# Second inputs of VectorE's selection steps in free PSUM columns, two key copies on ScalarE, zero rows written on chip, x loaded ahead by four columns

## The chip, the cores and the metric

The kernel runs on one core of one Trainium2 chip. The metric is the device time of one execution in microseconds (us), as the median of three runs. The core has TensorE (PE, matrix products, which write only to PSUM), VectorE (DVE), ScalarE (ACT) and GpSimd (POOL), and a queue of DMAs that SyncE (SP) issues in order.

## What is computed

For four sequences of 12,608 positions and 128 channels, a long convolution with a filter that a small network makes, gated by x; then, in each sequence, the 128 positions with the highest gate score pass through one expert and are written back.

```python
h = np.maximum(pos_emb @ w1, 0.0) @ w2 * np.exp(-0.01 * pos)[:, None]
u = x * v
y = irfft(rfft(u, n=2*S, axis=1) * rfft(h, n=2*S, axis=0)[None], n=2*S, axis=1)[:, :S]
a = x * y                                     # B, S, D = 4, 12608, 128
scores = a @ w_gate
for b in range(B):
    top = np.argpartition(-scores[b], 128)[:128]
    e = a[b, top]
    a[b, top] = e + sigmoid(scores[b, top])[:, None] * (np.maximum(e @ moe_w1, 0.0) @ moe_w2)
```

## The kernel before, in words

The Fourier transforms are matrix products of lengths 101 and 250. After a setup that makes the filter's spectrum (h_hid, h_spec; up to about 114 us), a loop takes one step t for four channels of one sequence: 32 steps a sequence (NG = 32), 128 in all. The order of all instructions is written out by hand; each engine works through its own queue in that order, and a framework adds the waits between engines.

In step t, in the order of the code (L1011 ff.): TensorE makes the inverse product of step t−3 (f_i, L254), then the second forward product of step t (dft, L259) into a PSUM tile of two banks, c0 for odd t and c1 for even t (404 of the 512 columns of each bank are used); ScalarE copies one half of it out (L262). TensorE then makes the first forward product of step t+1 (f_s1, L417), which ScalarE copies (L419). VectorE multiplies with the spectrum for step t−1, which still lies in the other PSUM tile (f_m, L431 and L432; f_y, L437 and L438), then combines step t (f_v, L426; f_u, L423). POOL makes sums and differences for f_i (f_sd, L444 and L445), the product x·v of a step ahead (L240) and a combination of results (f_c, L486 and L487). SP loads x and v of step t+4 (L234) and the spectrum (L244). The dft of step t+1 overwrites the PSUM tile from which L437 and L438 of step t−1 read.

After the 32 steps of a sequence comes its x-stage (P1): the last inverse product (L532, L536), the product with x (L547), the gate's weights (L581), and the row sums on ScalarE (L591). The first five blocks of x, eight columns each (420 KB), are loaded ahead into the buffers xa by load_a, one every second step at i%32 = 20, 22, ..., 28, where i = t−3 (LA, L44). 23 of the 128 rows of the xa buffers hold no data; at t=8 two DMAs write zeros from memory into them (460 KB, L1031).

The selection of the 128 rows of a sequence runs behind the steps of the next sequence, as a generator (topk_one, L973) that stands still at each `yield` until a step reaches a hook of that kind: "p" right after the dft, "n" behind it (no operation of its own: it only says that the next operation waits for a later step), "d" four times between L426 and L423, "e" three times at the step's end, after L423. With s = t mod 32 the background of a sequence starts at s=3: late row sums at s=3 and 4; at s=5 the mask (L594, a minimum of scores and table) and the sign step of the keys (L662); at s=6 the xor (L664), the copy of the keys' upper half (L665) and that of the lower half (L743). Then sixteen rounds of counting, one a step: ScalarE counts (L755), TensorE sums over the partitions (L250), VectorE compares (L761). After the eighth, at s=15, low() makes the second key on ScalarE (L746) and VectorE adds the lower half (L748). select (L780) follows: is_gt and is_equal at s=25 (L790, L793), TensorE's count and, at s=26, a copy (L806), a running sum (L808) and a comparison (L811), at s=27 an add (L814), at s=28 a second running sum (L817) and a product (L820), at s=29 two one-column operations in "d" hooks (L835, L837) and two comparisons (L839, L842), at s=30 the matmul of rows that reads L842's result (place, L250). The gather of the rows on POOL's DMA queue stands at a last hook. A running sum is one scan over 126 columns. All inputs of these steps, but sums straight from TensorE, lie in SBUF. For the last sequence (b = 3) the selection runs at the end, with nothing beside it.

f_last (L448) is the last step's spectrum product in two halves, the second of which has its sums on VectorE (L458, L459).

## Time and profile before

| | us |
|---|---|
| median of three runs | 921.66 (918.89 to 922.53) |
| the profiled execution | 915.3 |
| its span, first to last instruction | 913.4 |

| engine | busy, us | share of the span |
|---|---|---|
| TensorE (PE) | 870.1 | 95% |
| VectorE (DVE) | 825.0 | 90% |
| GpSimd (POOL) | 765.2 | 84% |
| ScalarE (ACT) | 620.7 | 68% |

The profile is of one execution. A share is a mean over the setup, the 128 steps, the four x-stages between them and the tail, which have different limits; a view by stretch gives the busy time of each engine in a part of the span. "Idle before" is the time in which an engine stood still ahead of an instruction, and the name behind the arrow is what ended it; "issue" stands for a wait that the profile does not explain. In the names of tiles the numbers are left out: "c" is a PSUM tile of two banks, "a" one of one bank, "arena" the large SBUF tile that holds most buffers.

### The profile page before, as it was taken

What the parts mean: (1) busy time and instruction counts of PE and PEld (TensorE: products, weight loads), DVE (VectorE), ACT (ScalarE), POOL (GpSimd) and SP (SyncE); (2) the same over time, 40 slices, a digit from 0 to 9 for tenths busy, and PEclk for the clock granted to TensorE, in tenths of its full rate; (3) what the DMA queues carried; (4) which work ended last, traced back from release to release, by engine and by line L of the source; (5) the groups of instructions that cost most, each with busy time, mean ns of one, the idle gap of its engine ahead of it and who ended that gap; (6) DMA issues with size and microseconds to landing.
All of it is one profiled execution on the core that took longest, in us unless ns stands there. A gap on an engine that the chain in (4) does not pass through costs nothing.

```text
span 913.4 us, 46302 instructions
## 1 busy us (share of the span) xinstructions
PE 870.1 (95%) x19606; PEld 748.2 (82%) x19606; DVE 825.0 (90%) x1543; ACT 620.7 (68%) x2226; POOL 765.2 (84%) x834
## 2 busy tenths in 40 slices
PE   8999899999999999999999999999999999989965
PEld 6878669899979878889798788887997788968954
DVE  8999799899999899999997999999998989997883
ACT  6665545555549969885579688955697888746920
POOL 5898569999999879898998798988997989979810
PEclk9999999999999999999999999999999999999997
DMA  7144587767879967677789676787797666855910
GB/s 246 39 184 170 193 296 192 248 208 225 256 220 285 306 179 229 194 237 230 234 244 300 208 222 196 229 234 240 231 295 236 203 207 207 249 167 168 296 55 7
DMA packets 80677, 195.52 MB, mean 214 GB/s; under 512 B 9302, under 2 KB 46271, under 8 KB 80447
## 3 DMA queue, kind: packets, MB, share of 16 engines
q1 hardware_dynamic: 80214, 192.04, 66.8%
q8 instruction: 154, 2.52, 1.1%
q0 software_dynamic: 256, 0.52, 0.2%
q14 instruction: 53, 0.43, 0.2%
HBM read 151.93 MB, written 40.60 MB: 211 GB/s over the span
## 4 chain that ended last, share of the span: by engine, by line
PE 53%; DVE 27%; ACT 11%; DMA 4%; issue 3%; POOL 3%; POOLq 0%; DVEq 0%; SPq 0%; ACTq 0%
PE c L254 15%; PE a L417 13%; PE c L259 12%; ACT arena L591 9%; DVE c L432 4%; DVE arena L431 4%; DVE arena L437 3%; DVE c L426 2%; DVE arena L438 2%; DVE c L423 2%; PE c L393 2%; PE a L373 2%; PE c L373 2%; DMA out_dram<-arena 1%; DMA hd<-arena 1%
## 5 line engine op out<-in xcount | busy, mean ns | idle before, releaser
L254 PE MATMUL c<-ci_sb,arena 128*26 128x126 f32 x8128 | 259.4, 270 | 5.3 <-issue 3.8
L254 PEld LDWEIGHTS c<-ci_sb,arena 128*26 128x26 f32 x8128 | 241.7, 104 | 10.1 <-issue 5.9
L259 PE MATMUL c<-arena,cf_sb 128*32 128x404 f32 x2048 | 211.9, 503 | 7.6 <-DVE arena L438 4.2
L417 PE MATMUL a<-c_sb,arena 128*32 128x202 f32 (+1 forms) x4096 | 214.3, 334 | 0.3 <-issue 0.3
L417 PEld LDWEIGHTS a<-c_sb,arena 128*32 128x32 f32 (+1 forms) x4096 | 167.4, 109 | 34.9 <-issue 15.2
L240 POOL TENSOR_TENSOR arena<-arena 128x500 f32<-128x500 f32 x128 | 162.5, 1270 | 12.4 <-DMA arena<-in_xg_dram 12.4
L444 POOL TENSOR_TENSOR arena<-arena 128x404 f32<-128x404 f32 x127 | 123.8, 974 | 54.0 <-DVE arena L438 39.6
L419 ACT COPY arena<-a 128x404 f32<-128x404 f32 x256 | 128.0, 500 | 52.8 <-PE a L417 50.9
L467 ACT COPY big<-c 128x824 f32<-128x824 f32 x127 | 106.3, 837 | 84.3 <-PE c L254 84.0
L591 ACT ACTIVATE arena<-arena 128x128 f32<-128x128 f32 x502 | 147.4, 297 | 11.4 <-DVE arena L581 9.5
L259 PEld LDWEIGHTS c<-arena,cf_sb 128*32 128x32 f32 x2048 | 93.0, 109 | 45.7 <-issue 24.4
L431 DVE TENSOR_TENSOR arena<-c,arena 128x808 f32<-128x808 f32 x127 | 126.6, 997 | 3.6
L432 DVE TENSOR_TENSOR c<-c,arena 128x808 f32<-128x808 f32 x127 | 126.6, 997 | 0.0
L445 POOL TENSOR_TENSOR arena<-arena 128x404 f32<-128x404 f32 x127 | 124.2, 978 | 0.0
L591 ACT ACTIVATION_READ_ACCUMULATOR arena<-arena 128x1 f32 x502 | 94.9, 189 | 0.0
L519 POOL TENSOR_TENSOR arena<-big 128x512 f32<-128x512 f32 x72 | 89.7, 1282 | 0.7 <-PE c L532 0.4
L262 ACT COPY arena<-c 128x404 f32<-128x404 f32 x128 | 63.5, 496 | 39.4 <-PE c L259 35.5
L426 DVE TENSOR_TENSOR c<-c,arena 128x404 f32<-128x404 f32 x128 | 74.6, 583 | 14.4 <-ACT arena L262 11.5
L437 DVE TENSOR_TENSOR arena<-c,arena 128x404 f32<-128x404 f32 x127 | 73.5, 579 | 12.9
L487 POOL TENSOR_TENSOR big<-big,arena 128x184 f32<-128x184 f32 x128 | 74.5, 582 | 10.0
L423 DVE TENSOR_TENSOR c<-c,arena 128x404 f32<-128x404 f32 x128 | 75.0, 586 | 2.7
L486 POOL TENSOR_TENSOR big<-big,arena 128x184 f32<-128x184 f32 x128 | 75.2, 587 | 0.0
(183 smaller groups left out, 1441.4 us busy)
## 6 DMA issues: line engine op xcount, KB each, us to landing
arena<-in_xg_dram SPq DMA_DIRECT2D x256, 250.0 KB, 3.7
arena<-hd SPq DMA_DIRECT2D x128, 404.0 KB, 4.4
arena<-in_x_dram SPq DMA_DIRECT2D x60, 420.0 KB, 4.8
out_dram<-arena SPq DMA_DIRECT2D x60, 420.0 KB, 5.5
hd<-arena SPq DMA_DIRECT2D x32, 404.0 KB, 3.0
arena<-in_pos_dram SPq DMA_DIRECT2D x15, 202.0 KB, 4.3
arena<-in_x_dram SPq DMA_DIRECT2D x4, 315.0 KB, 4.0
out_dram<-arena SPq DMA_DIRECT2D x4, 315.0 KB, 5.2
```

The lines of the kernel that those rows point to most:

```text
L240: nc.gpsimd.tensor_tensor(out=x, in0=x, in1=v, op=ALU.mult)
L254: nc.tensor.matmul(o[32 * k:32 * k + c.stop - c.start], lhsT=lhsT[:, c], rhs=rhs, start=True, stop=True)
L259: nc.tensor.matmul(pq[w][a:a + 32], lhsT=cf_sb[:, 2 * w + a // NQ, a % NQ:a % NQ + 32], rhs=te[:, a // NQ], start=True, stop=True)
L417: nc.tensor.matmul(tps[s // 2][c, s % 2], lhsT=u[:, s, c], rhs=c1_sb[:, 0:k + 2:k + 1], start=True, stop=True)
L419: nc.scalar.copy(out=te[:, :, 2 * h:2 * h + 2].rearrange("p e s i -> p s e i"), in_=tps[h])
L431: nc.vector.tensor_tensor(out=mt, in0=uv, in1=ht[:, 0].unsqueeze(1).to_broadcast([128, 2, HC]), op=ALU.mult)
L432: nc.vector.tensor_tensor(out=uv, in0=uv, in1=ht[:, 1].unsqueeze(1).to_broadcast([128, 2, HC]), op=ALU.mult)
L437: nc.vector.tensor_tensor(out=yz[:, 0], in0=uv[:, 1], in1=mt[:, 0], op=ALU.add)
L444: eng.tensor_tensor(out=nat(sd[:, 0]), in0=nat(yz[:, 0]), in1=rev(yz[:, 1]), op=ALU.add)
L445: eng.tensor_tensor(out=nat(sd[:, 1]), in0=rev(yz[:, 0]), in1=nat(yz[:, 1]), op=ALU.subtract)
L467: nc.scalar.copy(out=ay[:, t % NG, :NJ + JM, ss], in_=o3[:, :, :NJ + JM].rearrange("p s x -> p x s"))
L591: nc.scalar.activation(out=x, in_=x, func=AF.Copy, accum_out=self.sc[:, j:j + 1])
```

## The change

Four things are changed.

First, operands of the selection for the first three sequences are moved from SBUF into PSUM columns that no product uses: `gap(k, n)` is a view of columns 404 to 404+n of both banks of tile c0 or c1, with the 126 columns laid out as two halves. The mask's table is copied there once, at t=2, by ScalarE (c1); the sign step's result, the keys' lower half, the marks of select and one comparison lie in c0. VectorE's operations there then have one input in SBUF and one in PSUM (the sign step: its output in PSUM). A running sum becomes two scans of 63 columns, the second starting from the first's last value.

Second, the copies of the keys' upper and lower halves go from VectorE to ScalarE, in one step with the xor, and a "n" between the sign step and the xor goes away.

Third, the zero rows are no longer loaded: at t=0, 1 and 2 ScalarE writes zeros over the five xa buffers, all 128 rows of 1024 columns. The table `zr` and its argument are gone.

Fourth, the five blocks of x are loaded ahead in ten pieces of four columns, one in each step at i%32 = 20 to 29.

Besides, f_last keeps the second half's difference in PSUM.

```diff
@@ -41,7 +41,7 @@
 NE = 3
-LA = range(32 - 12, 32 - 2, 2)
+LA = range(32 - 12, 32 - 2)
 NS, ND = 64, 4
@@ -139,7 +139,7 @@
-    return (fold.astype(f), c1.astype(f), gx.astype(f), cf.astype(f), ci.astype(f), wm, tk, np.zeros((128 - P0 - PR, NX * 8 * D), f))
+    return (fold.astype(f), c1.astype(f), gx.astype(f), cf.astype(f), ci.astype(f), wm, tk)
@@ -192,6 +192,12 @@
         return view(bank2[k], 0, shape)
...
+    def gap(k, n):
+        return bank2[k].rearrange("p (c x) -> p c x", c=2)[:, :, HC:HC + n]
...
+    def c3(a):
+        return a.rearrange("p (c x) -> p c x", c=2)
@@ -206,6 +212,7 @@
     negm = tk_sb[:, 294:294 + NJ]
+    negp, tmp = gap(1, NJ // 2), gap(0, NQ)
     nst = tk_sb[:, 294 + NJ:].rearrange("p (r c) -> p r c", c=4)
@@ -454,9 +461,10 @@
             nc.vector.tensor_tensor(out=y[:, 0], in0=u[:, 1], in1=m[:, 0], op=ALU.add)
-            nc.vector.tensor_tensor(out=y[:, 1], in0=m[:, 1], in1=u[:, 0], op=ALU.subtract)
-            eng.tensor_tensor(out=d[:, 0], in0=y[:, 0], in1=y[:, 1, :, ::-1], op=ALU.add)
-            eng.tensor_tensor(out=d[:, 1], in0=y[:, 0, :, ::-1], in1=y[:, 1], op=ALU.subtract)
+            z = u[:, 0] if a else y[:, 1]
+            nc.vector.tensor_tensor(out=z, in0=m[:, 1], in1=u[:, 0], op=ALU.subtract)
+            eng.tensor_tensor(out=d[:, 0], in0=y[:, 0], in1=z[:, :, ::-1], op=ALU.add)
+            eng.tensor_tensor(out=d[:, 1], in0=y[:, 0, :, ::-1], in1=z, op=ALU.subtract)
         return sd
@@ -500,13 +508,14 @@
-        def load_a(self, i):
+        def load_a(self, i, a=0, z=8):
             if i < len(ORD):
...
                 j0, j1 = blocks[k]
+                z = min(z, j1 - j0)
                 o = i % (NX + len(XE))
                 self.xa[k] = buf("xa", o, [128, 8, D]) if o < NX else view(arena, XE[o - NX], [128, 8, D])
-                nc.sync.dma_start(self.xa[k][P0:P0 + PR, :j1 - j0], x2[self.b, :, j0:j1])
+                nc.sync.dma_start(self.xa[k][P0:P0 + PR, a:z], x2[self.b, :, j0 + a:j0 + z])
@@ -591,7 +600,8 @@
         def mask(self):
-            nc.vector.tensor_tensor(out=self.sc, in0=self.sc, in1=negm, op=ALU.min)
+            sc, m = (self.sc, negm) if self.last else (c3(self.sc), negp)
+            nc.vector.tensor_tensor(out=sc, in0=sc, in1=m, op=ALU.min)
@@ -714,8 +724,6 @@
                         if not self.ex:
-                            if k == 1:
-                                yield "n"
                             yield "e"
@@ -737,15 +745,23 @@
             self.cand = nst[:, 8]
-            self.lo = buf("ws", 0, [128, self.n])
+            self.lo = gap(0, self.n // 2)
         def split(self):
-            return super().split() + [lambda: nc.vector.tensor_copy(self.lo, self.half(U16, 0))]
+            V, sc, m = nc.vector, c3(self.sc.bitcast(I32)), self.lo.bitcast(I32)
...
+            def keys():
+                V.tensor_tensor(out=sc, in0=sc, in1=m, op=ALU.bitwise_xor)
+                nc.scalar.copy(out=self.key, in_=self.half(I16, 1))
+                nc.scalar.copy(out=self.lo, in_=c3(self.half(U16, 0)))
...
+            return [lambda: V.tensor_scalar(out=m, in0=sc, scalar1=31, scalar2=0x7FFFFFFF, op0=ALU.arith_shift_right,
+                                            op1=ALU.bitwise_and), keys]
...
             yield "e"
-            nc.vector.tensor_tensor(out=self.f, in0=self.f, in1=self.lo, op=ALU.add)
+            nc.vector.tensor_tensor(out=c3(self.f), in0=c3(self.f), in1=self.lo, op=ALU.add)
             self.key, self.cand = self.f, nst[:, 9]
@@ -784,40 +800,46 @@
         sn, rk = ws[:, o:o + n], ws[:, o + 2 * n:o + 3 * n + 2]
-        ev, oh = ws[:, o + n:o + 2 * n], ws[:, 128:256]
+        last = b + 1 == B
+        ev, oh = ws[:, o + n:o + 2 * n] if last else gap(0, n // 2), ws[:, 128:256]
+        w3 = (lambda a: a) if last else c3
         nc.scalar.activation(out=rk[:, n + 1:n + 2], in_=rs, func=AF.Copy, bias=float(b * PR * NJ))
...
+        def scan(initial):
+            for x, y in ((sn, ev),) if last else ((sn[:, h * n // 2:(h + 1) * n // 2], ev[:, h]) for h in range(2)):
+                nc.vector.tensor_tensor_scan(out=x, data0=one.to_broadcast([128, x.shape[1]]), data1=y, initial=initial,
+                                             op0=ALU.mult, op1=ALU.add)
+                initial = x[:, x.shape[1] - 1:]
...
         yield "e"
...
         yield "e"
-        nc.vector.tensor_scalar(out=ev, in0=k.f, scalar1=th, scalar2=0.0, op0=ALU.is_equal, op1=ALU.add,
+        nc.vector.tensor_scalar(out=ev, in0=w3(k.f), scalar1=th, scalar2=0.0, op0=ALU.is_equal, op1=ALU.add,
                                 accum_out=cnt[:, 1:2])
-        if b + 1 == B:
-            nc.vector.tensor_tensor_scan(out=sn, data0=one.to_broadcast([128, n]), data1=ev, initial=0.0, op0=ALU.mult,
-                                         op1=ALU.add)
+        if last:
+            scan(0.0)
         yield "p"
...
         mm2(ps[:, 0:1], tr, cnt[:, 1:2], start=False, stop=True)
-        if b + 1 == B:
+        if last:
             warm(3)
         yield "e"
-        if b + 1 < B:
+        if not last:
             nc.vector.tensor_copy(lim, ps[:, 0:1])
             yield "e"
-            nc.vector.tensor_tensor_scan(out=sn, data0=one.to_broadcast([128, n]), data1=ev, initial=lim,
-                                         op0=ALU.mult, op1=ALU.add)
+            scan(lim)
             yield "e"
-            nc.vector.scalar_tensor_tensor(out=ev, in0=sn, scalar=CAP + 0.5, in1=ev, op0=ALU.is_lt, op1=ALU.mult)
+            nc.vector.scalar_tensor_tensor(out=ev, in0=c3(sn), scalar=CAP + 0.5, in1=ev, op0=ALU.is_lt, op1=ALU.mult)
             yield "n"
             yield "e"
-            nc.vector.tensor_tensor(out=ev, in0=gt, in1=ev, op=ALU.add)
+            nc.vector.tensor_tensor(out=ev, in0=c3(gt), in1=ev, op=ALU.add)
             yield "n"
             yield "e"
-            nc.vector.tensor_tensor_scan(out=sn, data0=one.to_broadcast([128, n]), data1=ev, initial=0.0, op0=ALU.mult,
-                                         op1=ALU.add)
+            scan(0.0)
             yield "e"
-            nc.vector.tensor_tensor(out=rk[:, :n], in0=sn, in1=ev, op=ALU.mult)
+            nc.vector.tensor_tensor(out=c3(rk[:, :n]), in0=c3(sn), in1=ev, op=ALU.mult)
             tot = sn[:, n - 1:n]
@@ -828,18 +850,18 @@
             warm(2)
-            nc.vector.tensor_tensor_scan(out=sn, data0=one.to_broadcast([128, n]), data1=ev, initial=0.0, op0=ALU.mult,
-                                         op1=ALU.add)
+            scan(0.0)
             nc.vector.tensor_tensor(out=rk[:, :n], in0=sn, in1=ev, op=ALU.mult)
...
         yield "e"
-        nc.vector.tensor_scalar(out=ws[:, :128], in0=iot, scalar1=rk[:, n:n + 1], scalar2=0.0, op0=ALU.is_ge,
+        ge, i3 = (ws[:, :128], iot) if last else (tmp, c3(iot))
+        nc.vector.tensor_scalar(out=ge, in0=i3, scalar1=rk[:, n:n + 1], scalar2=0.0, op0=ALU.is_ge,
                                 op1=ALU.add, accum_out=cnt[:, 1:2])
         yield "e"
-        nc.vector.scalar_tensor_tensor(out=oh, in0=iot, scalar=en, in1=ws[:, :128], op0=ALU.is_lt, op1=ALU.mult)
+        nc.vector.scalar_tensor_tensor(out=w3(oh), in0=i3, scalar=en, in1=ge, op0=ALU.is_lt, op1=ALU.mult)
         return rk, oh
@@ -1026,9 +1048,11 @@
             load_u(t + NU)
-            if t == 8:
-                for r, z in ((0, P0), (P0 + PR, 128)):
-                    nc.sync.dma_start(arena[r:z, OFF["xa"][0]:OFF["xa"][0] + NX * 8 * D], zr[:z - r])
+            for k in range(2 * t, min(2 * t + 2, NX)):
+                nc.scalar.activation(out=buf("xa", k, [128, 8 * D]), in_=one.to_broadcast([128, 8 * D]), func=AF.Copy,
+                                     scale=0.0)
+            if t == 2:
+                nc.scalar.copy(out=negp, in_=c3(negm))
             o = t - 1 in uv
@@ -1070,7 +1094,8 @@
                 ph[b] = P1(b)
-            ph[b].load_a(LA.index(i % NG))
+            k, e = divmod(LA.index(i % NG), 2)
+            ph[b].load_a(k, e * HB, (e + 1) * HB)
         if i % NG == NG - 1 and i >= 0:
```

## Rows read from the trace of the kernel before

**Rows 1.** The page's first part: engine, busy us, share of span, instructions.
```profile
...
PE 870.1 (95%) x19606; PEld 748.2 (82%) x19606; DVE 825.0 (90%) x1543; ACT 620.7 (68%) x2226; POOL 765.2 (84%) x834
...
```

**Rows 2.** By stretch, t=12-27: us, PE, PEld, DVE, ACT, POOL busy, clock, DMA, GB/s.
```profile
...
168.25:239.46 71.21, 71.21 (x1797) 66.50 (x1791) 66.16 (x96) 40.87 (x80) 66.28 (x79) 1.00 0.75 224
...
```

**Rows 3.** Busy time by stretch: selection steps, first batch, and sum over three batches.
```profile
...
322.53:342.85 20.32, 18.35 (x465) 14.68 (x460) 19.67 (x33) 13.37 (x37) 15.97 (x19) 1.00 0.57 167
...
374.21:383.49 9.28, 9.28 (x242) 7.79 (x237) 8.95 (x18) 7.42 (x23) 9.12 (x11) 1.00 0.60 194
...
414.87:439.11 24.24, 23.42 (x608) 20.63 (x603) 23.48 (x40) 12.77 (x25) 19.80 (x24) 1.00 0.79 229
...
sum 167.18, PE 157.96 PEld 130.89 DVE 161.79 ACT 104.50 POOL 137.87; mean PE 17.55 PEld 14.54 DVE 17.98 ACT 11.61 POOL 15.32
```

**Rows 4.** Timeline of a plain step: start us, us, engine, line, [idle before <-releaser].
```profile
...
218.81 0.56 DVE L438 TENSOR_TENSOR arena<-arena,c 128x404 f32<-128x404 f32 x1
219.00 0.49 ACT L262 COPY arena<-c 128x404 f32<-128x404 f32 x1 [0.30 <-PE c L259]
...
220.77 1.00 DVE L431 TENSOR_TENSOR arena<-c,arena 128x808 f32<-128x808 f32 x1
...
221.66 0.50 PE L259 MATMUL c<-arena,cf_sb 128*32 128x404 f32 x1
...
```

**Rows 5.** Timeline, TensorE at t=40.
```profile
...
333.39 0.55 PE L259 MATMUL c<-arena,cf_sb 128*32 128x404 f32 x4 [1.70 <-DVE arena L438]
```

**Rows 6.** Timeline around t=62: slots of the selection, and who waits.
```profile
...
433.92 0.15 DVE L835 COPY arena<-a 128x1 f32<-128x1 f32 x1
...
434.05 0.58 DVE L423 TENSOR_TENSOR c<-c,arena 128x404 f32<-128x404 f32 x1
...
434.54 0.34 DVE L839 TENSOR_SCALAR_CACHE_REDUCE arena<-tk_sb,arena 128x128 f32<-128x128 f32 x1
434.60 0.96 POOL L445 TENSOR_TENSOR arena<-arena 128x404 f32<-128x404 f32 x1
...
434.93 0.78 DVE L842 SCALAR_TENSOR_TENSOR arena<-tk_sb,sel,arena 128x128 f32<-128x128 f32 x1
...
435.76 0.43 PE L250 MATMUL a<-arena 128*32 128x64 f32 x16 [0.53 <-DVE arena L842]
...
```

**Rows 7.** VectorE's groups by line and shape | busy us, mean ns | idle before.
```profile
...
L743 DVE CAST arena<-sc 128x126 f32<-128x126 uint16 x3 | 3.9, 1308 | 0.0
...
L811 DVE SCALAR_TENSOR_TENSOR arena<-arena 128x126 f32<-128x126 f32 x3 | 3.5, 1173 | 0.1
...
L808 DVE TENSOR_TENSOR_SCAN arena<-one,sel,arena 128x126 f32<-128x126 f32 x3 | 3.3, 1104 | 0.1
...
L817 DVE TENSOR_TENSOR_SCAN arena<-one,arena 128x126 f32<-128x126 f32 x3 | 1.3, 442 | 0.0
...
```

**Rows 8.** Line L581: duration ns min/median/max, first and last start us, shapes.
```profile
...
L581 DVE TENSOR_TENSOR arena<-arena,c x91: 421/677/680, 274.9 to 866.5; 128x512 f32<-128x512 f32 x88, 128x256 f32<-128x256 f32 x3
...
```

**Rows 9.** Timeline around t=48: low() on ScalarE and VectorE.
```profile
...
369.61 0.40 ACT L746 ACTIVATE f<-hi,st 128x126 f32<-128x126 int16 x1
...
369.75 0.51 PE L259 MATMUL c<-arena,cf_sb 128*32 128x404 f32 x2
...
370.04 0.85 DVE L748 TENSOR_TENSOR f<-f,arena 128x126 f32<-128x126 f32 x1 [1.17 <-ACT f L746]
...
```

**Rows 10.** Busy time by stretch: t=10, and t=88.
```profile
...
157.51:163.79 6.28, 4.90 (x125) 4.45 (x120) 5.87 (x10) 2.56 (x5) 6.20 (x8) 1.00 1.00 323
593.57:599.25 5.68, 4.77 (x126) 4.08 (x117) 5.29 (x11) 3.46 (x11) 5.60 (x7) 1.00 0.95 284
...
```

**Rows 11.** Timeline of TensorE within t=10.
```profile
...
162.91 0.31 PE L254 MATMUL c<-ci_sb,arena 128*25 128x126 f32 x4 [1.38 <-issue]
```

**Rows 12.** Timeline of ScalarE at t=1.
```profile
...
119.90 0.50 ACT L262 COPY arena<-c 128x404 f32<-128x404 f32 x1 [1.68 <-PE c L259]
```

**Rows 13.** VectorE's groups by line and shape, as rows 7: the last step.
```profile
...
L459 DVE TENSOR_TENSOR arena<-arena 128x202 f32<-128x202 f32 x1 | 0.7, 748 | 0.0
...
```

4 lines of the change are left out of this document (2 added, 2 removed).

## The prediction

> **What bounds the kernel now.** I read the page first. TensorE is busy 95% of the span [rows 1], VectorE 90%, GpSimd 84%; so I asked for stages, not shares. A stretch of sixteen steps without background work takes 71.21 us, all of it PE [rows 2]: 4.45 us a step, set by TensorE. VectorE is busy 66.16 us there, 4.13 a step: it runs in time but has only 0.32 us a step to spare, so whatever the selection adds to VectorE is not free, it is a debt paid back at 0.32 us a step.
>
> Then I priced the steps in which the selection runs against 4.45 (s is t mod 32; the background starts at s=3). Nine stretches, 34 steps, take 167.18 us [rows 3]; 34 × 4.45 is 151.3, so 15.9 us is lost there, in the same three places for each of three batches; the first batch's stretches stand as examples: making the keys and the first round (s=6 to 9) 20.32 − 17.80 = 2.5 us, low() with its aftermath (s=17, 18) 9.28 − 8.90 = 0.4, select (s=26 to 30) 24.24 − 22.25 = 2.0. The other two batches lose about 3.0, 0.4 and 2.0.
>
> How a debt becomes lost time: in a plain step [rows 4] L438 ends at 219.37, and the dft that overwrites the same PSUM tile starts two dfts on, 221.66: VectorE may be 2.3 us late before PE waits. After the keys it is later: PE stands 1.70 us for L438 [rows 5]. After the slots it is L842 that PE's row matmul waits for, 0.53 us [rows 6].
>
> Why VectorE is late: the operations are short but stretched. The scan L808 takes 1104 ns, the like scan L817 takes 442; L811 1173, L743 1308 on 126 columns [rows 7]. L842 shows what stretches them: it starts at 434.93 while POOL's L445 runs from 434.60 for 0.96, and ends 0.15 us after that ends [rows 6]. An operation with one PSUM input isn't stretched: 91 of L581 have median 677 and maximum 680 ns for 512 columns and 421 for 256 [rows 8], while POOL is busy 84% of the span [rows 1] and chance alone would stretch some. That is one ns a column, so about 0.29 us at 126.
>
> **The change part by part.**
>
> **Second inputs in PSUM, and one "n" fewer.** Every listed operation comes to about 0.29 us; of a scan cut in two each half lies between 0.22 (half of 442) and 0.44, I take 0.30. Key copies L665 and L743 leave VectorE. Without the "n" mask, sign step and xor all run at s=5, and everything after comes one step earlier, the gather DMA on POOL's queue too (off the path: its result is used in the tail).
> At s=5 VectorE does 3 × 0.29, then its next main operation, L431, waits for ScalarE's copy into the same PSUM tile: two ScalarE copies follow the xor, each at most 0.40 (L746, 126 columns [rows 9]) and, by L262's 0.49 for 404 [rows 4], hardly under 0.2: 0.4 to 0.8 together, 0.6 taken. Behind L431 stands the whole main chain. Debt 0.9 + 0.6 = 1.5; under 2.3, so the 1.70 us wait goes. What is late next is the first round's counts, on ScalarE behind VectorE's debt: I leave 0.3 us in each of the two batches that lose more, and 0.5 for PE stalls in these stretches that are not of VectorE (of the kind of t=10 below): 1.1 of the 15.9 stays.
>
> **The new wait: a shared tile.** The free columns lie in tile c0, whose first 404 columns per bank the dft of every odd t overwrites. The trace of before doesn't show whether PE must wait for a VectorE operation on other columns of the tile. From below: by columns, no wait, 0. From above: by tile, PE waits until the operation ends. Nearest row: ScalarE's L262 copies the half of the tile that PE writes first, yet sits idle 0.30 us until the last matmul of the other half [rows 4]. That is a wait coarser than columns, so I take the upper end.
> The Trainium skill, page "PSUM — Partial Sum Buffer", section "PSUM bank collisions raise a hardware error", says the same from the other side: guard PSUM by bank and quadrant, not by address, since two engines in one bank collide whichever columns they touch. No run here shows a collision. By that rule the sum is the one I take; without it it would be 5.4 us lower.
>
> Which operations meet it: those at even s, as the next dft then is odd. VectorE's hook operations start where L431 stands at 220.77, and the dft comes at 221.66: 0.9 us of room.
> - s=14, L748: it starts when L746 is through, 370.04, after the dft at 369.75 would have begun (one step later now, same place in the step) [rows 9]. At 0.29 it ends 0.58 behind: stall 0.6. What before paid at s=18 for its 0.85 is in the 15.9.
> - s=24, is_gt and is_equal: like L839, 0.39 from its start to L842's [rows 6], 0.8 together: no stall.
> - s=25 is odd: two half scans, L811 and a copy of one column (0.15, like L835 [rows 6]), 1.1; less 0.32, debt 0.8. s=26, the add: 0.8 + 0.29 − 0.9 = stall 0.2.
> - s=27 odd: half scans and L820, 0.9; debt 1.4. s=28: less 0.32, and from L835 to L842's end, without the main L423 between (0.49), 0.5 + 0.29 [rows 6]: 1.1 + 0.8 − 0.9 = stall 1.0.
> Sum 1.8 a batch, 5.4 in three.
>
> **Zero rows on chip.** At t=10 a step takes 6.28 with the DMA engines at share 1.00 [rows 10]; PE stops 1.38 us in mid-group with "issue" [rows 11], waiting for nothing the trace shows; I read that as its instructions coming late behind the zero DMAs issued at t=8. All of 6.28 − 4.45 = 1.8 goes. The five ScalarE writes of 1024 columns, at most 1.25 us each (from 0.49 for 404, L262 [rows 4]), stand at t=0 to 2, two a step; ScalarE has 1.68 us idle before L262 there [rows 12], so L262 is late by up to 0.8. VectorE waits for L262, and at t=2 also for the negp copy into c1, some 1.1 us. Before the first full step nothing is close on its heels; cover is the 2.3 us above. I take 0; uncovered it is 0.8.
>
> **x by four columns.** The same bytes in twice as many SP issues, one a step from s=23. At t=88, behind an x load, a step takes 5.68 with DMA share 0.95 [rows 10]: 1.2 lost. Half-size pieces leave less in front of PE's code; between 0 and 1.2 I take 0.6.
>
> **f_last.** L459, 748 ns, with two SBUF inputs [rows 13], comes to about half for its 202 columns (L581 at 256 takes 421 [rows 8]): up to 0.38 off if PE waits for it, 0 if not; 0.25 taken.
>
> Sum: 15.9 − 1.1 − 5.4 + 1.8 + 0.6 + 0.25 = 12.0 us off. The profiled execution took 915.3 (span 913.4 and 1.9 around it), 6.4 under the median of 921.66; it would come to 903.3. The other executions differ by waits I can't see, so I take the 12.0 off the median: 909.7.
>
> **The rivals.**
> 1. No wait by tile. For it: PE and VectorE touch different columns. Against it: L262's idle time. The 5.4 and the 1.1 come back and x gives 1.2: 19 off, 902.5. Chance 0.2.
> 2. The operations stay stretched, because one SBUF input is enough to be held up. Against it L581's narrow spread. Only the two copies moved (L743's 1.3 us of VectorE's debt and at most as much for L665: some 2 us of stall a batch) and the DMA parts stay, less the new waits: 6 + 2.7 − 5.4 = 3 off, 918.5. Chance 0.08.
> 3. The waits by tile cost twice what I make of them (10.8 for 5.4), and L431 at s=5 some 0.7 a batch: 12.0 − 5.4 − 2.1 = 4.5 off, 917. Chance 0.06.
> 4. Slower: every even-s operation makes PE wait as long as VectorE gets late. Place: the dft after s=14, 24, 26 and 28, twelve waits. Price: up to the 2.3 us of the plain lag each, 27 us in place of 5.4: 22 more, 931. It decides from 12p > 12.0 + 5.4 + 4.6, p = 1.8 us a wait. For it: VectorE's debt did reach 2.3 at L842. Against it: shorter operations make less debt. Chance 0.05.
> A stall doesn't cost the clock here: the granted clock is 1.00 (2.4 GHz) in all stretches with stalls [rows 3, 10].
>
> **How the numbers follow.** Forecast (stalls by tile, about 12 off) 0.61; rivals 0.2, 0.08, 0.06, 0.05. Range 901 to 918.5: it takes in rivals 1 to 3 and leaves out rival 4; the lower end lies 1.5 under rival 1, as medians of three here move by some ±1.8. About 0.5%, 4.6 us, is what a measurement can tell: faster beyond it the forecast's 0.61, rival 1's 0.2 and half of rival 3, 0.84; within it rival 2 and the other half, 0.11; slower rival 4, 0.05.
>
> **What would show it.** Right: the operations named at about 0.3 us, L743's copy on ScalarE, no wait of PE for L438 near s=8, PE's dft waiting for a VectorE selection operation at s=14 and 28, no stall at t=10. Wrong: dfts that start on time at s=15 and 29 (rival 1), stretched operations (rival 2), L431 waiting over 2 us for ScalarE at s=5, or PE stalls "issue" as often as before (then zero rows and x were not their cause).

## The result, and the profile after

| | us |
|---|---|
| kernel before, beside it | 920.27 median (915.86 to 922.53, 4 runs) |
| changed kernel | 908.2 median (905.24 to 909.9, 4 runs) |
| ratio | 0.9871, 95% interval 0.9822 to 0.9921 |
| profiled execution of the changed kernel | 909.53, span 907.8 |

The change takes 12.1 us off the median; the prediction was 909.7, 12.0 off. In a later series (below) the same kernel took 906.81 beside 922.17, ratio 0.9838 [0.9815, 0.9862].

In what follows line numbers are those of the changed kernel: L254 is now L261 (f_i), L259 is L266 (dft), L417 is L424, L262 is L269, L431, L432, L437 and L438 are L438, L439, L444 and L445 (so L438 names another line now), L743 became ScalarE's L756, L746/L748 are L762/L764, L808 is one call of the scan L810, L811 is L834, L814 is L837, L820 is L842, L839/L842 are L861/L864, L459 is L466.

The page's first part, as [rows 1]: VectorE has lost 16.5 us of busy time, ScalarE gained 5.9, TensorE has the same work.

```profile
...
PE 869.9 (96%) x19606; PEld 760.9 (84%) x19606; DVE 808.5 (89%) x1543; ACT 626.6 (69%) x2238; POOL 763.5 (84%) x834
...
```

By stretch, columns as in [rows 2]: the same 34 steps as in [rows 3], first batch and sum of three.

```profile
...
325.78:344.22 18.44, 18.36 (x464) 14.95 (x460) 17.29 (x33) 15.36 (x49) 16.81 (x21) 1.00 0.66 198
376.41:385.38 8.97, 8.97 (x240) 7.45 (x236) 8.55 (x17) 7.68 (x26) 8.81 (x12) 1.00 0.69 226
416.81:440.65 23.84, 23.12 (x596) 19.42 (x589) 22.94 (x47) 12.77 (x25) 20.91 (x26) 1.00 0.79 238
...
sum 157.41, PE 155.16 PEld 129.38 DVE 149.84 ACT 111.78 POOL 141.93; mean PE 17.24 PEld 14.38 DVE 16.65 ACT 12.42 POOL 15.77
```

And the step s=14, which was not in [rows 3]: first batch, and sum of three.

```profile
...
362.15:367.46 5.31, 4.96 (x132) 4.37 (x122) 3.90 (x10) 4.55 (x15) 5.07 (x6) 1.00 0.71 213
...
sum 15.64, PE 14.60 PEld 12.82 DVE 11.40 ACT 13.36 POOL 15.12; mean PE 4.87 PEld 4.27 DVE 3.80 ACT 4.45 POOL 5.04
```

34 steps went from 167.18 to 157.41, 9.8 less. Keys and first round (s=6 to 9) went from 20.32 to 18.44, almost the 17.80 that TensorE needs; low()'s two steps from 9.28 to 8.97; select's five only from 24.24 to 23.84. The step s=14 takes 5.31, where a plain step takes 4.45. The timeline around its end (start us, us, engine, line, [idle before <-releaser]) shows why: VectorE's add L764 in tile c0 starts when ScalarE's L762 is through, as before [rows 9], but now the dft waits for it and starts as it ends.

```profile
...
366.68 0.40 ACT L762 ACTIVATE f<-hi,st 128x126 f32<-128x126 int16 x1
367.11 0.29 DVE L764 TENSOR_TENSOR f<-f,c 128x126 f32<-128x126 f32 x1 [1.17 <-ACT f L762]
...
367.46 0.89 PE L266 MATMUL c<-arena,cf_sb 128*32 128x404 f32 x8 [0.35 <-DVE f L764]
...
```

The step loses more (0.86 us) than the wait that is listed (0.35), because it loses an overlap as well: a step earlier the dft began at 362.15, while the last matmuls of f_i ran on to 362.56; here it begins after them.

The same at the end of s=28, where the last two comparisons stand: the dft stands 0.72 us for L864.

```profile
...
430.60 0.34 DVE L861 TENSOR_SCALAR_CACHE_REDUCE c<-tk_sb,arena 128x128 f32<-128x128 f32 x1
...
431.03 0.35 DVE L864 SCALAR_TENSOR_TENSOR arena<-tk_sb,sel,c 128x128 f32<-128x128 f32 x1
...
431.53 1.56 PE L266 MATMUL c<-arena,cf_sb 128*32 128x404 f32 x16 [0.72 <-DVE arena L864]
...
```

VectorE's groups by line and shape, as [rows 7]: everything is near the time that was taken for it, half a scan 345 ns (0.30 us taken), the sign step 293, the product 288; f_last's L466 takes 366 in place of 748 [rows 13].

```profile
...
L810 DVE TENSOR_TENSOR_SCAN arena<-one,arena,c 128x63 f32<-128x63 f32 x6 | 2.1, 345 | 0.2
...
L758 DVE TENSOR_SCALAR c<-sc 128x126 int32<-128x126 int32 x3 | 0.9, 293 | 0.1
...
L842 DVE TENSOR_TENSOR arena<-arena,c 128x126 f32<-128x126 f32 x3 | 0.9, 288 | 0.1
...
L466 DVE TENSOR_TENSOR arena<-arena,c 128x202 f32<-128x202 f32 x1 | 0.4, 366 | 0.0
...
```

The step t=10 and the one at t=88, as [rows 10]: both are plain now.

```profile
...
160.69:165.15 4.46, 4.46 (x122) 4.12 (x117) 4.29 (x7) 2.55 (x5) 4.38 (x6) 1.00 0.73 229
595.06:599.51 4.45, 4.45 (x120) 4.16 (x115) 4.31 (x11) 2.66 (x6) 4.19 (x6) 1.00 0.69 183
...
```

### The profile page after: what moved, and what is told of

Same layout as the page of the kernel before. It is cut to its first block, busy times and chain, and to the rows that moved or that the text cites. A ratio compares the mean times of both kernels' runs of the same rounds, so it can differ in the third digit from the quotient of the medians.

```text
span 907.8 us, 46386 instructions
## 1 busy us (share of the span) xinstructions
PE 869.9 (96%) x19606; PEld 760.9 (84%) x19606; DVE 808.5 (89%) x1543; ACT 626.6 (69%) x2238; POOL 763.5 (84%) x834
## 4 chain that ended last, share of the span: by engine, by line
PE 62%; DVE 18%; DMA 8%; ACT 6%; issue 3%; POOL 2%; POOLq 0%; SPq 0%; DVEq 0%; ACTq 0%
PE c L261 20%; PE a L424 16%; PE c L266 16%; ACT arena L600 4%; DMA hd<-arena 4%; DVE arena L408 3%; PE c L545 2%; DMA out_dram<-arena 2%; PE a L541 2%; PE a L545 2%; DMA arena<-in_x_dram 2%; DVE arena L438 2%; DVE c L439 2%; PE c L541 1%; DVE ms L694 1%
## 5 line engine op out<-in xcount | busy, mean ns | idle before, releaser
L261 PE MATMUL c<-ci_sb,arena 128*26 128x126 f32 (+1 forms) x8128 | 260.6, 271 | 3.9 <-DVE arena L556 2.7
L261 PEld LDWEIGHTS c<-ci_sb,arena 128*26 128x26 f32 (+1 forms) x8128 | 243.0, 104 | 8.8 <-DVE arena L556 3.2
L266 PE MATMUL c<-arena,cf_sb 128*32 128x404 f32 x2048 | 213.0, 505 | 6.5 <-DVE arena L864 2.2
L424 PE MATMUL a<-c_sb,arena 128*32 128x202 f32 (+1 forms) x4096 | 214.8, 334 | 0.0
L424 PEld LDWEIGHTS a<-c_sb,arena 128*32 128x32 f32 (+1 forms) x4096 | 173.5, 108 | 28.1 <-issue 12.8
L426 ACT COPY arena<-a 128x404 f32<-128x404 f32 x256 | 127.8, 499 | 53.3 <-PE a L424 52.4
L266 PEld LDWEIGHTS c<-arena,cf_sb 128*32 128x32 f32 x2048 | 98.9, 109 | 41.7 <-issue 24.0
L438 DVE TENSOR_TENSOR arena<-c,arena 128x808 f32<-128x808 f32 x127 | 126.8, 999 | 5.3 <-ACT c L756 1.6
L439 DVE TENSOR_TENSOR c<-c,arena 128x808 f32<-128x808 f32 x127 | 126.7, 998 | 0.0
L269 ACT COPY arena<-c 128x404 f32<-128x404 f32 x128 | 63.5, 496 | 34.9 <-PE c L266 29.4
L444 DVE TENSOR_TENSOR arena<-c,arena 128x404 f32<-128x404 f32 x127 | 73.6, 579 | 12.9
```

What stands on the lines that cost most here:

```text
L261: nc.tensor.matmul(o[32 * k:32 * k + c.stop - c.start], lhsT=lhsT[:, c], rhs=rhs, start=True, stop=True)
L266: nc.tensor.matmul(pq[w][a:a + 32], lhsT=cf_sb[:, 2 * w + a // NQ, a % NQ:a % NQ + 32], rhs=te[:, a // NQ], start=True, stop=True)
L424: nc.tensor.matmul(tps[s // 2][c, s % 2], lhsT=u[:, s, c], rhs=c1_sb[:, 0:k + 2:k + 1], start=True, stop=True)
L426: nc.scalar.copy(out=te[:, :, 2 * h:2 * h + 2].rearrange("p e s i -> p s e i"), in_=tps[h])
L438: nc.vector.tensor_tensor(out=mt, in0=uv, in1=ht[:, 0].unsqueeze(1).to_broadcast([128, 2, HC]), op=ALU.mult)
L439: nc.vector.tensor_tensor(out=uv, in0=uv, in1=ht[:, 1].unsqueeze(1).to_broadcast([128, 2, HC]), op=ALU.mult)
```

## Experiments

Each ratio is against the kernel before, run beside it; its median was 920.64 us in the first series (the next four), 922.17 in the second (the four after these), 922.28 in the third (the next three) and 921.68 in the last. The ratio is the recorded estimate and not the quotient of the two medians, from which it differs by up to 0.0022; "off" in us is worked out from the ratio.

**The selection's part alone.** The changed kernel, its zero rows and x loaded as before:

```diff
-LA = range(32 - 12, 32 - 2)
+LA = range(32 - 12, 32 - 2, 2)
...
-            for k in range(2 * t, min(2 * t + 2, NX)):
-                nc.scalar.activation(out=buf("xa", k, [128, 8 * D]), in_=one.to_broadcast([128, 8 * D]), func=AF.Copy,
-                                     scale=0.0)
+            if t == 8:
+                for r, z in ((0, P0), (P0 + PR, 128)):
+                    nc.sync.dma_start(arena[r:z, OFF["xa"][0]:OFF["xa"][0] + NX * 8 * D], zr[:z - r])
...
-            k, e = divmod(LA.index(i % NG), 2)
-            ph[b].load_a(k, e * HB, (e + 1) * HB)
+            ph[b].load_a(LA.index(i % NG))
```

> The changed kernel with the zero rows again loaded by the two DMAs at t=8 and x again in five blocks of eight columns: what is left is the selection's PSUM operands, the key copies on ScalarE and f_last. My sum gives this part 15.9 - 1.1 - 5.4 + 0.25 = 9.7 us of the 12.0, so about 910.5 against a kernel before at about 920, with the 1.8 us stall at t=10 back. Rival A, the DMA parts carry most of the gain: 916 or more. Rival B, x in ten pieces costs time (its steps at s=3 and the x-stage are longer in the changed kernel) and the DMA parts together give nothing: 908 or less, at or under the changed kernel.

Measured: 908.77 (906.09 to 912.39), ratio 0.9871 [0.984, 0.9902], so 11.9 us off, between 9.0 and 14.7. Rival A falls. My 9.7 lies in the interval; whether the DMA parts are worth 0 (rival B) or 2.4 this run can't tell.

**Everything one step later.** One "n" back between sign step and xor:

```diff
+                        yield "n"
                         yield "e"
```

> The changed kernel with one "n" put back between the sign step and the xor: everything of the selection from the xor on comes one step later, so operations on tile c0 that stood in even steps stand in odd ones and the other way round. Theory, PE waits by tile, not by columns: the waits of the changed kernel at s=14 (0.65 to 0.85 us), 26 (0.35) and 28 (1.0) go; L764 at s=15 is followed by a dft into c1 and costs nothing; new waits stand where the half scans and the comparison now lie, s=26 about 0.4 and s=28 about 0.6; net about 1.2 us a batch, 3.5 to 4.5 us off the changed kernel, about 904. Rival, PE waits there because VectorE is late, whatever tile it works on: the step s=15 stalls as s=14 did, and the time stays at 908.

Measured: 906.5 (902.55 to 907.35), 0.9824 [0.9795, 0.9853]. By stretch, the steps s=14, 15, 26 and 28 of the first batch:

```profile
...
360.86:365.35 4.49, 4.49 (x127) 4.45 (x121) 4.21 (x9) 3.98 (x14) 4.22 (x6) 1.00 0.65 199
365.35:369.83 4.48, 4.48 (x125) 4.48 (x118) 3.50 (x8) 3.80 (x13) 4.23 (x6) 1.00 0.76 224
414.63:419.97 5.34, 5.12 (x140) 4.64 (x131) 5.10 (x11) 2.72 (x6) 4.69 (x7) 1.00 0.85 273
424.42:429.51 5.09, 4.69 (x121) 3.76 (x113) 4.88 (x10) 2.90 (x6) 4.79 (x7) 1.00 0.77 240
...
```

The step s=14 is plain again and so is s=15, in which L764 now stands: the wait went with the tile and not with VectorE's lateness. New waits stand at s=26 and 28, as foreseen, but of 0.89 and 0.64 us, not 0.4 and 0.6. The net is some 0.6 us a batch, and the time fell by less than these series can tell.

**Operands back in SBUF**, with the order, ScalarE's copies and the DMA parts of the changed kernel:

```diff
-            sc, m = (self.sc, negm) if self.last else (c3(self.sc), negp)
+            sc, m = self.sc, negm
...
-            self.lo = gap(0, self.n // 2)
+            self.lo = c3(buf("ws", 0, [128, self.n]))
...
-        ev, oh = ws[:, o + n:o + 2 * n] if last else gap(0, n // 2), ws[:, 128:256]
+        ev, oh = ws[:, o + n:o + 2 * n] if last else c3(ws[:, o + n:o + 2 * n]), ws[:, 128:256]
...
-        ge, i3 = (ws[:, :128], iot) if last else (tmp, c3(iot))
+        ge, i3 = (ws[:, :128], iot) if last else (c3(ws[:, :128]), c3(iot))
```

> The changed kernel with its order, its key copies on ScalarE, its half scans, zero rows and x pieces, but the second inputs of the selection's VectorE operations (mask, sign step, lower half, marks, comparison) back in SBUF. Theory, two SBUF inputs are stretched beside POOL's work and PSUM ones are not: the mean times of mask, sign step, xor, half scans, products and comparisons rise from 0.28 to 0.35 us to between 0.5 and 1.2 us; the tile waits at s=14, 26 and 28 go as such, but VectorE's debt is back, 2 to 3 us in select and 1 to 2 at the keys in each batch: 911 to 915. Rival, it was the order and the copies on ScalarE that gained and not the place of the operands: 908 or, as the tile waits go, as low as 902.

Measured: 916.34 (911.18 to 925.04), 0.9941 [0.9916, 0.9965], a little slower than the theory had it. The place of the operands is worth some 6 to 9.5 us (0.9941 against the changed kernel's 0.9871 in the result and 0.9838 in the series below); what is left is what the two DMA parts gave alone (0.9941, below), so order and ScalarE's copies by themselves gave nothing that shows. The traces say the same: the 81 steps from s=6 to the next x-stage, in three batches, take 377.9 us here, 378.2 and 377.3 in the two profiles of the kernel before, and 371.1 and 370.9 in those of the changed kernel. VectorE's groups of this kernel:

```profile
...
L810 DVE TENSOR_TENSOR_SCAN arena<-one,arena 128x63 f32<-128x63 f32 x9 | 7.2, 796 | 0.2
...
L842 DVE TENSOR_TENSOR arena<-arena 128x126 f32<-128x126 f32 x3 | 3.5, 1179 | 0.1
...
L758 DVE TENSOR_SCALAR arena<-sc 128x126 int32<-128x126 int32 x3 | 3.5, 1165 | 0.1
...
L815 DVE TENSOR_SCALAR_CACHE_REDUCE arena<-f,st 128x126 f32<-128x126 f32 x4 | 1.4, 338 | 0.1
...
```

Half scans take 796 ns and the product 1179, where they take 345 and 288 from PSUM. The sign step L758 has one SBUF input and is held up all the same; its output lies in SBUF here. The comparison L815, which also counts, is not. The Trainium skill, page "SBUF — State Buffer", section "Who interferes with whom", sorts them in the same way: two SBUF inputs contend with a GpSimd instruction that reads SBUF, as can copies and tensor_scalar in modes that use both port pairs, but not the form that also writes its accumulator. The rows agree for these lines.

**All operations on c0 in odd steps**, so that the dft behind each writes c1:

```diff
+                        yield "n"
                         yield "e"
...
             nc.vector.tensor_copy(lim, ps[:, 0:1])
+            yield "n"
             yield "e"
             scan(lim)
             yield "e"
             nc.vector.scalar_tensor_tensor(out=ev, in0=c3(sn), scalar=CAP + 0.5, in1=ev, op0=ALU.is_lt, op1=ALU.mult)
-            yield "n"
             yield "e"
             nc.vector.tensor_tensor(out=ev, in0=c3(gt), in1=ev, op=ALU.add)
             yield "n"
+            yield "n"
             yield "e"
...
         nc.vector.tensor_tensor(out=en, in0=t, in1=tot, op=ALU.add)
+        if not last:
+            yield "n"
         yield "e"
```

> The changed kernel with "n"s so placed that every VectorE operation of the selection that touches tile c0 stands in an odd step (s=15, 25, 27, 29, 31), whose following dft writes c1. Theory, waits by tile: no dft waits for a selection operation any more, some 2.3 us a batch come back, about 7 us, so about 901. Rival, the waits come from VectorE's debt: spreading gives less than 2 us, 906 to 908. Rival, a later end of the selection costs something else (the gather and the place products come up to two steps later, near the x-stage): 908 or more.

Measured: 905.5 (903.36 to 909.8), 0.9821 [0.9792, 0.985]. TensorE's waits (what it waited for: us in total, times, longest):

```profile
...
PE c L261 <- issue: 2.9, 4, 1.4
...
PE c L257 <- ACT arena L476: 1.9, 1, 1.9
...
```

The waits for L764 and L864 are gone, and in this execution the 81 steps from s=6 on are 6 us shorter (365.0), yet the time didn't fall by 7 us. 1.9 us stand in the tail, where the third batch's row matmul now comes after the last step, and "issue" has appeared in the steps, most of it at s=5 (1.4 and 0.8 us). The two profiles of the changed kernel have no "issue" wait of over 0.15 us in the steps; the first lists these among others:

```profile
...
PE c L266 <- DVE arena L864: 2.2, 3, 0.7
...
PE c L266 <- ACT arena L426: 1.8, 2, 1.1
...
PE c L266 <- DVE f L764: 1.0, 3, 0.3
...
```

**The changed kernel again**, beside the variants of the second series.

> The changed kernel once more, unaltered, so that it stands beside the variants of this series: about 908 as before if its first four times are typical. By the theory that each tile wait costs what the trace shows (2.0 to 2.3 us a batch at s=14, 26 and 28, three batches), the kernel without them of this series should lie about 6 us lower; by the rival that the time only moves to other waits, less than 2 us.

Measured: 906.81 (905.71 to 907.99), 0.9838 [0.9815, 0.9862], span of the profiled execution 903.9.

**Odd steps, and the DMA parts as before** (the edits of the first and the fourth variant together).

> The changed kernel with all of VectorE's operations on tile c0 in odd steps, and with the zero rows and x loaded as in the kernel before. The kernel with the selection part alone took 908.8 us. Theory, the tile waits are worth what the trace shows (about 2.2 us a batch) and the two DMA parts are worth nothing together: about 902. Rival, the DMA parts are worth the 2.4 us of my sum: 904 to 905. Rival, the tile waits' time moves to other waits: 907 to 909.

Measured: 907.88 (905.66 to 910.28), 0.9846 [0.982, 0.9873]: the rival, the time moves. TensorE's waits:

```profile
...
PE c L261 <- issue: 4.1, 7, 1.1
...
PE c L257 <- ACT arena L476: 1.5, 1, 1.5
...
```

In the first batch's select this kernel has 2.3 us of "issue" in three stalls and no wait for L864; the kernel with the selection's part alone, which differs only in the "n"s, has 0.7 us for L864 there and no "issue". Of the 4.1 us, 1.1 are the stall at t=10 that comes with the zero table.

**Zero rows alone**, on the kernel before (the diff is that of the change).

> The kernel before with its zero rows written by ScalarE at t=0 to 2, and nothing else. My sum: 1.8 us off, about 918.5 against a kernel before at 920.5; the step t=10 takes 4.45 instead of 6.28. Rival: the four kernels without the zero table run their first matmuls (6.7 to 11 us after the start) at half the pace and come 1.5 to 2.0 us later out of that stretch, the two with it don't; if that hangs on the zero rows, this kernel starts late as well, t=10 is won and the start is lost: 920 to 921.

Measured: 919.83 (916.2 to 924.71), 0.9988 [0.9965, 1.0012]. The step t=10 by stretch:

```profile
...
157.51:161.96 4.45, 4.45 (x122) 4.08 (x116) 4.23 (x8) 2.56 (x5) 4.37 (x6) 1.00 0.70 226
...
```

The stall of [rows 10] is gone, and it goes with the zero table in every profile: t=10 takes 5.93 to 6.39 us in the five that have the table and 4.45 in the nine that don't. The rival isn't settled. In its strict form it falls: its profile did start late, but so did that of the odd kernel with the zero table, and the changed kernel's second profile didn't (see the last section). But seven of the nine profiles without the table started late and one of the five with it, and the time lies between the two forecasts.

**x in pieces alone.**

> The kernel before with x loaded in ten pieces of four columns, and nothing else. My sum: 0.6 us off (0 to 1.2), so 919.5 to 920.5, with no stall near t=88. Rival: the pieces end later, so that the x-stage and the first steps after it are longer, 48.3 us for x-stage and s=3 in the mean of twelve batches of kernels with pieces against 47.6 in six with blocks, some 0.7 us a batch: 921 to 923. In both cases the first matmuls run at full pace if the late start hangs on the zero rows.

Measured: 917.78 (914.25 to 923.83), 0.9962 [0.9937, 0.9987]: 3.5 us off, between 1.2 and 5.8, where I had 0.6; the rival, a longer time, falls. t=88 takes 4.48, without a stall; t=10 stays:

```profile
...
156.99:163.03 6.04, 4.83 (x124) 4.34 (x116) 5.75 (x10) 2.56 (x5) 5.96 (x8) 1.00 0.99 326
...
```

**Odd steps, third batch earlier** (the last "n" only for the first two batches).

> The kernel with all operations on c0 in odd steps took 905.5 us and not the 901 expected: its tile waits are gone, but in its third batch the row matmul comes after the last step and waits 1.5 to 1.9 us for ScalarE there, and the tail is 99.4 us long in place of 95.8 to 97.4. Here the third batch leaves out the last "n" (its two comparisons stand at s=30 and PE waits some 0.25 us there). Theory, the tail was what ate the gain: tail back at 96 to 97.5, the time 1.5 to 2 us lower, about 903.7, and 0.980 to 0.981 of the kernel before. Rival, the tail varies from run to run: about 905.5 again.

Measured: 906.26 (902.56 to 909.95), 0.9826 [0.979, 0.9862]. TensorE's waits:

```profile
...
PE c L261 <- issue: 3.6, 5, 1.3
...
PE c L266 <- DVE arena L868: 1.1, 1, 1.1
...
PE a L261 <- DVE ix L890: 1.0, 1, 1.0
...
```

The tail is 96.5 us long again, but the third batch's two comparisons at s=30 cost TensorE 1.1 us of wait and not 0.25 (that step takes 6.16), another 1.0 follows in the tail (L890, the rows' index), and "issue" is at 3.6.

**Both DMA parts**, on the kernel before.

> The kernel before with the zero rows written on chip and x in ten pieces, nothing else. My sum gave the two parts 2.4 us. Alone they measured 1.1 us (zero rows, between -1.1 and 3.2) and 3.5 us (x, between 1.2 and 5.8) off. Theory, they stand beside each other and beside the selection: 4 to 5 us off, a ratio of about 0.995. Rival, they save the same stalls: 2 to 3.5 us off. Rival, the value of x was chance: 1 to 2.4 off.

Measured: 917.94 (912.67 to 922.37), 0.9941 [0.9915, 0.9967]: 5.4 us off, between 3.0 and 7.8. By the ratios they add up and are worth more than my 2.4; by the medians alone it would be 2.3 (zero rows), 4.4 (x) and 4.3 us (both), so whether they add up is open. With the selection's 11.9 the 5.4 makes 17.3, above the 12.1 and 15.4 of the whole, within the intervals of the parts. The profile of this kernel has as much "issue" in its steps as the kernel before, 2.2 us of it at s=27 to 29 of the first batch, beside the x pieces:

```profile
...
PE c L254 <- issue: 4.1, 5, 1.4
...
```

**The kernel before again.**

> The kernel before once more, unaltered, for a second profiled execution: the first took 915.3 us, at the fast end of its runs (medians of 920.3 to 922.2). If the usual execution differs from it by TensorE stalls that the profile calls "issue", this one, at 919 to 923 us, shows 4 to 8 us more of them than the 4.1 us in the steps of the first, in steps with x loads (s=23 to 31) or just behind an x-stage (s=3 to 6); if it differs by the pace of the first matmuls, 1.5 to 2 us of it lie in the first 12 us; if by the clock, the granted clock is lower than 0.991.

Measured: 921.12 (916.89 to 929.78), 0.9996 [0.9968, 1.0024]; the profiled execution took 925.68. TensorE at its last step, t=127, and then the granted clock (columns here: us, TensorE's busy time, clock, DMA share, GB/s; a clock of 1.00 is 2.4 GHz, 0.50 is 1.2):

```profile
...
823.64 0.55 PE L259 MATMUL c<-arena,cf_sb 128*32 128x404 f32 x4 [2.16 <-issue]
```

```profile
...
821.00:825.00 4.00, 1.84 (x20) 1.00 0.59 170
825.00:830.00 5.00, 3.79 (x133) 1.00 0.02 3
830.00:835.00 5.00, 3.84 (x72) 0.70 0.55 147
835.00:840.00 5.00, 5.00 (x60) 0.61 0.15 42
...
```

A 2.16 us stall of "issue" just ahead of the tail, and a granted clock of 0.70 and 0.61 in the mean of two windows of 5 us, after a stretch in which TensorE was busy 5.6 of 9 us: 5 × 0.30 + 5 × 0.39 = 3.4 us. Together that is the 5.6 us by which the tail, from the last dft on, is longer (103.1 against 97.4), more than half of the 10.3 between the two spans. The "issue" waits in the steps are 3.3 us against 4.1 in the first profile; so the other executions don't simply have more of them.

**Odd steps, a quarter of the x bytes.** Of each four-column piece one column is loaded; three quarters of the block loads ahead are left out.

```diff
-                nc.sync.dma_start(self.xa[k][P0:P0 + PR, a:z], x2[self.b, :, j0 + a:j0 + z])
+                nc.sync.dma_start(self.xa[k][P0:P0 + PR, a:a + 1], x2[self.b, :, j0 + a:j0 + a + 1])
```

> The kernel with all operations on c0 in odd steps and the early end of the third batch (906.3 us), with one column of each four-column piece of x loaded ahead instead of four: three quarters of these bytes are left out, so its output isn't the reference's. With the tile waits gone, the profiled executions of the odd kernels show TensorE stalls of "issue" (2.9 to 4.4 us in the steps, most at s=28 and 30) which the two profiles of the changed kernel don't show. Theory, the stalls are TensorE's instructions coming late behind the x transfers, and the tile waits only hid them: without the bytes they go from the steps s=20 to 31, and the time falls by what the tile waits were worth, 3 to 6 us, to 900 to 903. Rival, they do not hang on the x transfers: as many as before, 905 to 907.

Measured: 901.37 (900.4 to 902.5), 0.9778 [0.9751, 0.9804]. No wait for "issue" is left in its steps. Steps s=28 to 30 of the first batch, first with the whole pieces, then with a quarter of them:

```profile
...
424.89:441.03 16.14, 14.43 (x360) 11.60 (x355) 15.51 (x27) 7.67 (x15) 13.90 (x17) 1.00 0.84 248
...
```

```profile
...
419.17:432.61 13.44, 13.44 (x352) 12.29 (x347) 12.85 (x22) 7.67 (x15) 11.18 (x15) 1.00 0.69 206
...
```

13.44 is three plain steps, with TensorE busy throughout. So in this order the "issue" stalls hang on the x transfers. With them gone the spread of the times is 2 us in place of 7; but the changed kernel's in the second series, with all the bytes, was 2.3. The larger gain lies elsewhere, in the three steps behind each x-stage (s=3 to 5; sum of three batches, again first with the whole pieces):

```profile
...
sum 45.99, PE 42.17 PEld 29.72 DVE 35.84 ACT 33.99 POOL 34.51; mean PE 14.06 PEld 9.91 DVE 11.95 ACT 11.33 POOL 11.50
```

```profile
...
sum 40.06, PE 40.06 PEld 31.20 DVE 31.70 ACT 34.19 POOL 32.37; mean PE 13.35 PEld 10.40 DVE 10.57 ACT 11.40 POOL 10.79
```

That is 5.9 us, of which 0.8 were "issue"; most of the listed rest is the dft behind s=3 waiting for a copy on ScalarE (L426).

## Why the prediction came out right, point by point

**The bound and the debt.** Right. The excess of the keys' steps over 4.45 fell from 8.6 us in three batches to 1.1, which is what I left there; low()'s to 0.2 (0 foreseen). L431's wait for ScalarE, now L438's, is 0.53 us, 0.6 foreseen:

```profile
...
326.27 0.30 ACT L755 COPY hi<-sc 128x126 int16<-128x126 int16 x1 [1.18 <-DVE sc L754]
...
326.47 0.26 ACT L756 CAST c<-sc 128x126 f32<-128x126 uint16 x1
...
326.76 1.00 DVE L438 TENSOR_TENSOR arena<-c,arena 128x808 f32<-128x808 f32 x1 [0.53 <-ACT c L756]
...
```

No dft waits for L445 (was L438) at s=8 any more, except once in the first batch for 0.8 us.

**Stretched operations.** Right, and the operands' place was the cause: some 6 to 9.5 us between the kernel and its copy with SBUF operands, about 7 of it in the 81 steps from s=6 on. Rival 2 falls.

**The wait by tile.** Right in kind: moving the operations by one step moved the waits, and in odd steps there are none. Rival 1 falls. The Trainium skill's rule of guarding PSUM by bank (page "PSUM — Partial Sum Buffer", section "PSUM bank collisions raise a hardware error") is what these rows look like; no run here shows a collision. The waits are ones that the framework adds for the tile; whether the chip would need them no run shows. In size I was short: s=14 costs 0.76 us in the mean of three (0.6 foreseen), s=26 0.35 (0.2), s=28 1.0 (1.0), together 6.4 us in three batches, not 5.4. Another 0.2 a batch at s=29 is no wait: the row matmul (L257, 16 matmuls) stands there now, and TensorE is busy all the time:

```profile
...
431.53:436.20 4.67, 4.67 (x128) 3.84 (x132) 4.50 (x10) 1.89 (x5) 4.09 (x6) 1.00 0.79 257
...
```

In the kernel before it stood at s=30 (5.44), so that 0.7 us of TensorE's own work lay in the 15.9 that my sum took for lost. Both together are 1.7 us: 1.2 of them in select, whose net gain is 1.2 us and not 2.4, and 0.5 at s=14. Rival 3's doubling and rival 4 fall.

By rows the selection is worth 180.64 − 173.05 = 7.6 us in the steps (34 steps and s=14, before and after), where my sum had 15.9 − 1.1 − 5.4 = 9.4; the difference is the tile waits' 1.0 and the row matmul's 0.7.

**Zero rows.** The 1.8 us at t=10 are gone, as foreseen. The writes take 1.06 us each (at most 1.25 foreseen) and hold nothing up, but at t=3 VectorE waits 0.69 for the mask table's copy and the step takes 4.72: 0.3 us that I had put at 0. Alone it measured 1.1 us off [-1.1, 3.2].

**x by four columns: the term that was mis-sized.** 0.6 taken, 1.2 the bound; alone it measured 3.5 [1.2, 5.8]. At t=88 the row says 5.68 → 4.45, 1.2 us, as the bound had it, but that is luck: in the second profile of the kernel before, with the whole blocks, the same step has no stall:

```profile
...
598.74:603.23 4.49, 4.49 (x126) 4.01 (x121) 4.21 (x9) 3.47 (x11) 4.41 (x6) 1.00 0.85 246
...
```

So the stall belonged to one execution, and I took both bounds from it (915.3 us, 6 us quicker than its own median). Nor is the mechanism shown, that half-size pieces end such stalls: with both DMA parts alone there are 2.2 us of them beside the pieces. No profile shows where the 3.5 us come from; x alone took 915.28 in its profiled execution, the kernel before 915.3 in its first. The cause stays open. One profile can't show a term that differs from execution to execution.

**f_last.** L466 is 0.38 us shorter; the tail went from 97.4 to 95.8 us, which varies by more than that.

**The step from the profile to the median.** I took the 12.0 off the median and not off the profiled 915.3, and that was right: the two profiled executions differ by 5.8 us alone. The changed kernel's lost about 3 us where the other didn't: its granted clock was 0.82 and 0.83 in the mean of two windows of 5 us behind the second x-stage (the trace's clock record has 0.50, 1.2 GHz, for 3.4 us there), some 1.7 us,

```profile
...
495.00:500.00 5.00, 3.10 (x72) 2.51 (x76) 3.75 (x7) 2.97 (x17) 3.19 (x3) 0.82 0.95 359
500.00:505.00 5.00, 5.00 (x112) 3.31 (x108) 2.50 (x5) 2.88 (x13) 4.23 (x6) 0.83 0.96 329
...
```

and about 1.3 us in its first matmuls (last section). Its second profile has neither, and its span of 903.9 is 9.5 us under the 913.4 of the kernel before. My sentence that a stall doesn't cost the clock here held for the stretches I had looked at. Behind an x-stage and at the start of the tail the clock did fall, in four of the fourteen profiles (in the last 30 us it falls in all of them), but not always behind a stall: the kernel with a quarter of the x bytes, which has no "issue", had 0.50 for 3.4 us there too. What makes it fall in one execution and not in another no run shows.

That 12.0 came out as 12.1 (15.4 in the second series) is in part luck. By rows the selection gave 1.8 us less than the sum had; by their own run the DMA parts gave 3 us more, between 0.6 and 5.4, at a place that no trace shows. But the selection's own run says 11.9 where the rows say 7.6. These accounts agree to some 4 us and no better, so that the two errors cancelled is likely, not shown.

**Where the tile waits' time goes.** Taking them away didn't pay: 905.5, 907.88 and 906.26 against 906.81 to 908.2. The profiled executions by stretch, in us, from the starts of the dfts (the first 34 steps and the x-stages, 278 to 283 together, are left out):

| kernel | setup | s=3 to 5, nine steps | s=6 on, 81 steps | tail | span |
|---|---|---|---|---|---|
| before | 114.7 | 41.4 | 378.2 | 97.4 | 913.4 |
| before again | 116.4 | 43.8 | 377.3 | 103.1 | 923.7 |
| changed | 117.5 | 43.6 | 371.1 | 95.8 | 907.8 |
| changed again | 114.6 | 42.9 | 370.9 | 97.3 | 903.9 |
| all odd | 118.3 | 45.8 | 365.0 | 99.4 | 908.0 |
| odd, third batch earlier | 115.4 | 46.0 | 368.7 | 96.5 | 908.2 |
| the same, a quarter of x | 114.7 | 40.1 | 365.6 | 99.8 | 899.9 |

Shown is that with all odd the 6 us did come in the steps where the tile waits had stood, and that the execution lost them behind the x-stages, in the tail and in the setup. Of that the wait in the tail (1.9 us) is due to the order; the setup differs by 2.9 us between two executions of the changed kernel. In the other two odd kernels "issue" stalls take part of the gain in the steps themselves. With a quarter of the x bytes the same order takes 901.4, most of it won at s=3 to 5. That the tile waits hide TensorE's late instructions is one reading: outside t=10, the three profiles with all of these waits have at most 0.4 us of "issue" before the last step, the ten others with all of x 1.7 to 4.1. It doesn't account for s=3 to 5; there the order and the x transfers can't be told apart, as a run of the changed kernel itself with a quarter of the x bytes was not made. No variant that loads all of x beats the changed kernel by more than its interval.

## What to carry to other kernels

Where VectorE runs beside a busy GpSimd, moving one of two SBUF inputs into spare PSUM columns makes a 126-column operation 0.3 us instead of 0.5 to 1.2, but a spare column is a tenant of its tile: the next matmul into that tile waits for it, so look which matmul comes next. Placing the operations ahead of a matmul into the other tile removed the waits here but no time that could be measured: what one stretch gains another can lose, so price a removed wait by the whole run. And size a term that depends on transfers from more than one execution.
